# A decode block bound by loading: fewer VectorE instructions, and w_down's row results summed by f32 products

## The chip, the cores and the metric

The kernel runs on one core of a Trainium2 chip. The metric is device time in microseconds (us) of one execution, the median of several runs. A profile comes from one execution. Its span leaves out part of the measured time, so spans and times are never mixed below.

Names used: PE is TensorE's matmul, PEld its weight load (they overlap: 320.5 and 208.1 us busy in a span of 437.8), DVE is VectorE, ACT ScalarE, POOL GpSimd, SP the engine that issues the loads. A "load" is one transfer from HBM; the trace records 16 landings for each of those of weights and cache, and the page counts 16 DMA engines.

## The reference

One decoding step of a transformer block: adaptive layernorm, attention of one query token over a cache of 65,536 positions (4 key/value heads, 32 query heads), then a gated FFN.

```python
def reference(A_x, A_k_cache, A_v_cache, A_wq, A_wo, B_x, B_w_gate, B_w_up, B_w_down, c, w_mod):
    mod = (_silu(c) @ w_mod).reshape(c.shape[0], 6, 1, -1)      # sa, ca, ga, sb, cb, gb
    h = _layernorm(x) * (1 + ca) + sa
    x = x + ga * attention(h)        # k_cache, v_cache: [1, 4, 65536, 128] bf16, 67 MB each
    h = _layernorm(x) * (1 + cb) + sb
    return x + gb * ((_gelu(h @ w_gate) * (h @ w_up)) @ w_down)  # w_down: [3584, 1024]
```

There is one token, so every weight and every cache entry is used once. 185.6 MB must be read.

## The kernel before

The kernel is written engine by engine. Each engine has a program of its own, and semaphores tie the engines together. The parts that the change and the argument touch follow; cuts are marked `# ...` or `...`; in the diffs below, a line in round brackets says what stands there.

The head: GpSimd builds constants and zeroes buffers; VectorE derives selection matrices, gives 40 semaphores their starting value, and zeroes two pads.

```python
pool.memset(p_row[:, :, :], 0.0)
# ...
v_zero = GP.done(pool.memset(kt_sb[:, 1, :, :], 0.0))       # 128 x 8192 bf16
DVE.wait(t1)
dve.memset(selw[:, :], 0.0)
v = DVE.done(dve.memset(q_buf[:, :, :], 0.0))
# ...
dve.tensor_scalar(selt[:, :].rearrange("p (r h) -> p r h", h=REP), identf[0:REP, 0:REP]..., -scale, None, ALU.mult)
# ...
sites = [a for r in ev for a in r] + ex + m1 + m2 + oc + pc + kfill + vfill
for a in sites:
    dve.sem_inc(a.sem, a.unit)
v_pad = DVE.done(dve.memset(s_pad[:, :, :], 0.0))
v_pads = DVE.done(dve.memset(h_pad[:, :, :], 0.0))
```

The loop: 32 steps of 64 x 128 keys. TensorE transposes K, VectorE and ScalarE copy it out, TensorE forms scores, and a running maximum is taken across partitions with two small f32 products (MT, MB) and several small VectorE operations.

```python
v = DVE.done(dve.tensor_reduce(m_new, sc(j), AX.X, ALU.max))
m1[s].done(dve.scalar_tensor_tensor(m_sp[:, j % 2, :], m_new.to_broadcast([P, NR]),
                                    m_run[:, 1 - j % 2:2 - j % 2], rsel[:, :], ALU.max, ALU.mult))
pt["mr"] = DVE.done(dve.tensor_tensor(m_run[...], m_run[...], m_new, ALU.max))
DVE.wait(pt[("MT", j)])
m2[s].done(dve.tensor_reduce(mg[:, j % 2:j % 2 + 1], b6[0:REP, 0:NR], AX.X, ALU.max))
DVE.wait(pt[("MB", j)])
v_mc[j] = DVE.done(dve.tensor_copy(mneg[:, j:j + 1], b6[:, 256:257]))
```

The tail, the w_down product. It has two forms. The "row" form streams 512 columns of w_down past the activations (in the trace a weight load of 128x32 and a product of 128x512), and leaves results in rows that must be turned into columns. The "column" form makes each 128 x 128 block of w_down the stationary operand and streams one column (a weight load of 128x128, a product of 128x1): 8 products for each 128 rows of w_down. The first loads to arrive ("early") use rows, the last four ("late") use columns. Rows are copied out of PSUM, turned by eight f32 transposes, reduced, scaled and added; the column results come on top.

```python
v = row_matvec(place_d, early, o_pad, (v_uc,), ...)
v_rows = both(row_a, 2, P)                              # PSUM -> SBUF, f32, on VectorE and ScalarE
v = turn(tr_ps, P, row_a, plain, P, v_rows)             # 8 f32 transposes of 128 x 128
v = DVE.done(dve.tensor_reduce(t_dn.unsqueeze(2), quads(tr_ps, KD), AX.X, ALU.add))
v = DVE.done(dve.tensor_tensor(t_dn, t_dn, gb_nat[:, :], ALU.mult))
v_base = DVE.done(dve.tensor_tensor(x1_nat[:, :], t_dn, x1_nat[:, :], ALU.add))
v = col_matvec(acc_dn, j_d[len(early):], o_pad[:, :, 0], (), KD)   # 64 products of the late loads
DVE.wait(v, v_base)
```

Of the kernel before, what the change touches and what calls it, by code (L numbers as in the profile page):

```python
# [6 lines left out]
ALU = mybir.AluOpType  # L7
AX = mybir.AxisListType
# [72 lines left out]
def bass_adaLN_cond__gqa_block_cached__geglu_ffn__decode_kernel(  # L81
# [76 lines left out]
    o_acc = sb("o_acc", [P, ROW])  # L158
    o_red = sb("o_red", [P, Hkv, P + 1])
    m_run = sb("m_run", [P, 2])  # L160
    NR = P // REP
    m_sp = sb("m_sp", [P, 2, NR])
    rsel = sb("rsel", [P, NR])
    mg = sb("mg", [REP, 2])
    selt = sb("selt", [REP, P])
    s_fp = s_pad[:, :, :].rearrange("p k c -> p (k c)").bitcast(dt.float32)
# [85 lines left out]
    def emit_all():  # L252
# [64 lines left out]
        while b < NBF:  # L317
# [12 lines left out]
        m1 = [Site(nc, f"m1_{s}") for s in range(SITES)]  # L330
        m2 = [Site(nc, f"m2_{s}") for s in range(SITES)]
        oc = [Site(nc, f"oc{s}") for s in range(SITES)]
# [12 lines left out]
        v_const = GP.done(pool.affine_select(  # L345
            spread[:, :], spread[:, :], [[1, P + QW - 1]], ALU.not_equal, 1.0, base=1 - QW, channel_multiplier=-QW))
        pool.memset(p_row[:, :, :], 0.0)
        pool.memset(p_sb[:, :, :], 0.0)
        pool.memset(m_sp[:, :, :], 0.0)
        pool.memset(mg[:, :], 0.0)  # L350
        pool.memset(slots[SITES + 1][:, 2 * M6 - SLOT:SLOT], 0.0)
        v_zero = GP.done(pool.memset(kt_sb[:, 1, :, :], 0.0))

        DVE.wait(t1)
        dve.memset(selw[:, :], 0.0)
        v = DVE.done(dve.memset(q_buf[:, :, :], 0.0))
        DVE.wait(v)
        dve.tensor_reduce(
            selw[:, HQ - REP:HQ].unsqueeze(2), identf[:, :].rearrange("p (r h) -> p h r", h=REP), AX.X, ALU.add)
        dve.tensor_reduce(  # L360
            rsel[:, :].unsqueeze(2), identf[:, :].rearrange("p (r h) -> p r h", h=REP), AX.X, ALU.add)
        dve.tensor_scalar(  # L362
            selt[:, :].rearrange("p (r h) -> p r h", h=REP),
            identf[0:REP, 0:REP].unsqueeze(1).to_broadcast([REP, NR, REP]), -scale, None, ALU.mult)
        v = DVE.done(dve.tensor_reduce(
            dm4.unsqueeze(3), identf[:, :].rearrange("p (c b h) -> p c b h", c=NQ, h=REP), AX.X, ALU.add))
        DVE.wait(v)
        v_sel = DVE.done(dve.tensor_reduce(
            dmask[:, :].unsqueeze(2), dm4.rearrange("p c b -> p b c"), AX.X, ALU.add))

        sites = [a for r in ev for a in r] + ex + m1 + m2 + oc + pc + kfill + vfill
        for a in sites:
            dve.sem_inc(a.sem, a.unit)

        v_pad = DVE.done(dve.memset(s_pad[:, :, :], 0.0))
        v_pads = DVE.done(dve.memset(h_pad[:, :, :], 0.0))
        PE.wait(t1, (c_sem, 32))
# [12 lines left out]
        v = DVE.done(dve.tensor_scalar(sg_col[:, :], th_col[:, :], 0.5, 0.5, ALU.mult, ALU.add))  # L390
        DVE.wait(v, v_pads)
        v_s = DVE.done(dve.tensor_tensor(s_pad[:, :, 0], c_col[:, :], sg_col[:, :], ALU.mult))

        def col_matvec(bank, jobs, rhs, ready, nblk):

            PE.wait(*ready)
            tok = None
            first = True
            for (jb, view, k0, nk) in jobs:
                PE.wait(jb.tok)  # L400
                ins = None
                for kk in range(nk):
                    for j in range(nblk):
                        ins = pe.matmul(
                            bank[:, j:j + 1], view[:, kk, j * P:(j + 1) * P], rhs[:, k0 + kk:k0 + kk + 1],
                            start=first, stop=True, skip_group_check=True,
                        )
                        first = False
                tok = PE.done(ins)
                release(jb, tok)  # L410
            return tok
# [150 lines left out]

        for s in range(SITES):
            v_q = DVE.done(q_set(s, 0))

# [20 lines left out]
        def pe_step(i, off=0):  # L586
# [48 lines left out]
            def MT():  # L635
                j = i - 1
                if not 0 <= j < NC:
                    return
                pwait(m1[j % SITES], j, it)
                ins = None  # L640
                if emit:
                    ins = pe.matmul(  # L642
                        b6[0:REP, 0:NR], selw[:, HQ - REP:HQ], m_sp[:, j % 2, :], start=True, stop=True)
                pt[("MT", j - off)] = PE.done(ins)

            def MB():
                j = i - 1
                if not 0 <= j < NC:
                    return
                pwait(m2[j % SITES], j, it)  # L650
                ins = None
                if emit:
                    ins = pe.matmul(  # L653
                        b6[:, 256:257], selt[:, :], mg[:, j % 2:j % 2 + 1],
                        start=True, stop=True,
                    )
                pt[("MB", j - off)] = PE.done(ins)

# [51 lines left out]
            MT()  # L710
            MB()

# [3 lines left out]
        def others_step(i):  # L716
# [11 lines left out]
            def OC():  # L728
# [3 lines left out]
                g, first, last = j // NCH, j % NCH == 0, j % NCH == NCH - 1  # L732
                z = o_red[:, g, P:P + 1]
                DVE.wait(pt[("PV", j)], v_x[j], pt.get("z"), pt.get("OC"))
                if first:
                    v = oc[j % SITES].done(dve.tensor_copy(o_acc[:, :], b7[:, :]))
                    pt["z"] = DVE.done(dve.tensor_copy(z, zr[:, j:j + 1]))
                else:
                    v = oc[j % SITES].done(dve.scalar_tensor_tensor(  # L739
                        o_acc[:, :], o_acc[:, :], al[:, j:j + 1], b7[:, :], ALU.mult, ALU.add))  # L740
                    pt["z"] = DVE.done(dve.scalar_tensor_tensor(z, z, al[:, j:j + 1], zr[:, j:j + 1], ALU.mult, ALU.add))
                pt["OC"] = v
                if last:
                    ov = o_acc[:, :].rearrange("p (b d) -> p b d", b=NB)
                    DVE.wait(v)
# [11 lines left out]
            if 0 <= j < NC:  # L757
                s, first = j % SITES, j % NCH == 0
                DVE.wait(pt[("QK", j)])
                if first:  # L760
                    pt["mr"] = v = DVE.done(dve.tensor_reduce(m_run[:, j % 2:j % 2 + 1], sc(j), AX.X, ALU.max))
                    DVE.wait(v)
                    m1[s].done(dve.tensor_scalar(
                        m_sp[:, j % 2, :], rsel[:, :], m_run[:, j % 2:j % 2 + 1], None, ALU.mult))
                else:
                    v = DVE.done(dve.tensor_reduce(m_new, sc(j), AX.X, ALU.max))  # L766
                    DVE.wait(v, pt["mr"])
                    m1[s].done(dve.scalar_tensor_tensor(  # L768
                        m_sp[:, j % 2, :], m_new.to_broadcast([P, NR]), m_run[:, 1 - j % 2:2 - j % 2],
                        rsel[:, :], ALU.max, ALU.mult))  # L770
                    pt["mr"] = DVE.done(dve.tensor_tensor(
                        m_run[:, j % 2:j % 2 + 1], m_run[:, 1 - j % 2:2 - j % 2], m_new, ALU.max))
                if j + SITES < NC and (j + SITES) // NCH != j // NCH:
                    q_set(s, (j + SITES) // NCH)
                DVE.wait(pt[("MT", j)])
                m2[s].done(dve.tensor_reduce(  # L776
                    mg[:, j % 2:j % 2 + 1], b6[0:REP, 0:NR], AX.X, ALU.max))
                DVE.wait(pt[("MB", j)])
                v_mc[j] = DVE.done(dve.tensor_copy(mneg[:, j:j + 1], b6[:, 256:257]))
            jt = i - 2  # L780
# [39 lines left out]
        for g in range(Hkv):  # L820
            ins = pe.matmul(
                b6[0:HQ, 0:P + 1], selw[:, HQ - REP * (g + 1):HQ - REP * (g + 1) + QD], o_red[:, g, :],
                start=g == 0, stop=g == Hkv - 1)
        v = PE.done(ins)
        DVE.wait(v)
        v = DVE.done(dve.reciprocal(rz[:, :], b6[0:HQ, P:P + 1]))
        DVE.wait(v)
# [91 lines left out]
        v_rows = both(row_a, 2, P)  # L919
        v = turn(tr_ps, P, row_a, plain, P, v_rows)  # L920
        DVE.wait(v)
        v = DVE.done(dve.tensor_reduce(t_dn.unsqueeze(2), quads(tr_ps, KD), AX.X, ALU.add))
        DVE.wait(v)
        v = DVE.done(dve.tensor_tensor(t_dn, t_dn, gb_nat[:, :], ALU.mult))
        DVE.wait(v)
        v_base = DVE.done(dve.tensor_tensor(x1_nat[:, :], t_dn, x1_nat[:, :], ALU.add))
        v = col_matvec(acc_dn, j_d[len(early):], o_pad[:, :, 0], (), KD)
        DVE.wait(v, v_base)
        v = DVE.done(dve.tensor_tensor(t_dn, acc_dn, gb_nat[:, :], ALU.mult))
# [42 lines left out]
```

## Time and profile before

439.15 us (439.04 to 439.38, six runs).

| reading | value | view |
|---|---|---|
| span | 437.8 us | page |
| bytes read, mean rate | 185.6 MB, 424 GB/s | page |
| VectorE busy | 50% | page |
| TensorE's waits for K loads in the loop | 28.5 us | waits |

First, lines of the page: DMA busy tenths and GB/s in 40 slices of the span, then three DMA queues (packets, MB, share of 16 engines' span).

```profile
DMA  8999999999999999999999999999999999999994
GB/s 358 433 420 437 436 442 433 430 427 431 434 434 434 432 431 432 431 431 431 431 431 431 431 431 434 432 443 440 440 431 431 431 428 421 439 423 443 414 428 204
q1 hardware_dynamic: 7904, 185.60, 98.6%
q8 instruction: 8, 0.13, 0.1%
q14 instruction: 5, 0.04, 0.0%
```

The rate hardly moves from the second slice to the last but one. The kernel is bound by loading.

The view of waits, TensorE's for K (engine and line, what it waited for, us in all, times, longest):

```profile
PE kt_ps L604 <- DMA slots<-in_A_k_cache_dram: 28.5, 12, 3.7
```

TensorE waits for loads in the loop, not loads for TensorE.

The timeline at the head (start, length, engine, line, operation; in brackets how long the engine had been idle and for whom):

```profile
3.11 12.32 DVE L362 TENSOR_SCALAR selt<-identf 8x128 f32<-8x128 f32 x1
8.44 6.92 POOL L352 MEMSET kt_sb<- 128x8192 bf16 x1
19.27 0.17 DVE L375 MEMSET s_pad<- 128x128 uint32 x1 [3.62 <-issue]
20.97 7.00 PE L427 MATMUL kt_ps<-slots,s_pad 128*32 128x512 bf16 x72
```

VectorE's tiny scaling into `selt` takes 12.32 us and ends at 15.43, when GpSimd's last memset does (15.36). Semaphore increments fill 15.65 to 19.27. The first w_mod products start at 20.97.

The timeline at the tail:

```profile
430.06 1.05 PE L427 MATMUL kt_ps<-slots,p_row 128*32 128x512 bf16 x8 [0.54 <-DMA slots<-in_B_w_down_dram]
431.18 0.69 DVE L845 COPY kt_sb<-kt_ps 128x512 f32<-128x512 f32 x1 [6.76 <-PE kt_ps L427]
431.93 1.97 PE L488 MATMUL sc_ps<-identf,kt_sb 128*128 128x128 f32 x8 [0.82 <-DVE kt_sb L845]
433.69 1.89 PE L404 MATMUL b<-p_row,slots 128*128 128x1 bf16 x64
435.62 0.17 DVE L929 TENSOR_TENSOR kt_sb<-b,gb_nat 128x8 f32<-128x8 f32 x1 [1.09 <-PE b L404]
```

The last early load is used at 430.06, rows are copied by 431.87, the transposes' weight loads run until 433.5, and the late column products end at 435.58.

### The profile page before, as it was taken

The numbers are of one execution on the slowest core, as the hardware profiler recorded it, in microseconds if no ns is written. First come the engines' busy times: TensorE is split into PE (matmuls) and PEld (weight loads), VectorE is DVE, ScalarE is ACT, GpSimd is POOL, SyncE is SP. The second block draws the span as 40 slices with busy tenths as digits, with TensorE's granted clock in tenths as the row PEclk, the third lists the DMA queues.
The fourth block names the chain that finished last, engine by engine and source line by source line (L and its number), as shares of the span: only waits on it lengthen the run. The fifth ranks groups of instructions, "written<-read, shape, count | busy, mean of one in ns | idle before, by whom it ended". The sixth has DMA issues, their size and how long they took to land.

```text
span 437.8 us, 8748 instructions
## 1 busy us (share of the span) xinstructions
PE 320.5 (73%) x3950; PEld 208.1 (48%) x3950; DVE 218.4 (50%) x407; ACT 111.8 (26%) x165; POOL 15.7 (4%) x20
## 2 busy tenths in 40 slices
PE   0156669879896887979697896979888695575466
PEld 0022336656564555655465564655556463232223
DVE  7501024656583746657375674647566475321101
ACT  1000001443332513433333343333235334000000
POOL 9400000000000000000000000000000000000000
PEclk9995558988896968999698898879889999577655
DMA  8999999999999999999999999999999999999994
GB/s 358 433 420 437 436 442 433 430 427 431 434 434 434 432 431 432 431 431 431 431 431 431 431 431 434 432 443 440 440 431 431 431 428 421 439 423 443 414 428 204
DMA packets 7937, 185.78 MB, mean 424 GB/s; under 512 B 882, under 2 KB 882, under 8 KB 1268
## 3 DMA queue, kind: packets, MB, share of 16 engines
q1 hardware_dynamic: 7904, 185.60, 98.6%
q8 instruction: 8, 0.13, 0.1%
q14 instruction: 5, 0.04, 0.0%
q10 hardware_dynamic: 20, 0.01, 0.0%
HBM read 185.60 MB, written 0.00 MB: 424 GB/s over the span
## 4 chain that ended last, share of the span: by engine, by line
DMA 54%; PE 32%; DVE 11%; issue 2%; ACT 1%; POOL 0%; DVEq 0%; POOLq 0%
DMA slots<-in_A_k_cache_dram 43%; PE kt_ps L604 15%; DMA slots<-in_B_w_down_dram 7%; PE b L687 5%; DMA slots<-in_A_v_cache_dram 4%; PE sc_ps L626 4%; PE kt_ps L427 3%; DVE selt L362 3%; DVE kt_sb L726 2%; DVE s_pad L766 1%; DVE o_red L749 1%; PE sc_ps L668 1%; PE sc_ps L488 1%; PE b L653 1%; DVE o_acc L739 1%
## 5 line engine op out<-in xcount | busy, mean ns | idle before, releaser
L604 PE MATMUL kt_ps<-ident,slots 128*128 128x128 bf16 x2048 | 156.6, 237 | 29.2 <-DMA slots<-in_A_k_cache_dram 28.5
L726 DVE COPY kt_sb<-kt_ps 128x2048 bf16<-128x2048 bf16 x96 | 117.5, 1224 | 91.6 <-PE kt_ps L604 87.6
L604 PEld LDWEIGHTS kt_ps<-ident,slots 128*128 128x128 bf16 x2048 | 134.0, 107 | 56.7 <-issue 39.9
L726 ACT ACTIVATE kt_sb<-kt_ps 128x2048 bf16<-128x2048 bf16 x32 | 60.1, 1877 | 28.7 <-PE kt_ps L604 28.7
L784 ACT ACTIVATE p_sb<-sc_ps 128x512 bf16<-128x512 bf16 x32 | 19.1, 597 | 179.8 <-PE sc_ps L668 179.8
L626 PE MATMUL sc_ps<-kt_sb,q_buf 128*32 128x512 bf16 x528 | 51.5, 425 | 0.0
L687 PE MATMUL b<-slots,p_sb 128*32 128x512 bf16 x560 | 43.8, 442 | 4.4 <-DMA slots<-in_A_v_cache_dram 3.7
L427 PE MATMUL kt_ps<-slots,h_pad 128*32 128x512 bf16 x176 | 19.9, 590 | 18.4 <-DMA slots<-in_B_w_up_dram 7.1
L739 DVE SCALAR_TENSOR_TENSOR o_acc<-o_acc,s_pad,b 128x512 f32<-128x512 f32 x28 | 20.9, 748 | 14.9 <-PE b L687 14.8
L687 PEld LDWEIGHTS b<-slots,p_sb 128*32 128x32 bf16 x560 | 16.4, 109 | 20.9 <-issue 8.3
L790 ACT ACTIVATE p_row<-sc_ps,s_pad 128x512 bf16<-128x512 f32 x32 | 21.7, 677 | 0.0
L642 PE MATMUL b<-m_sp,selw 128*8 128x16 f32 x66 | 6.9, 180 | 18.5 <-DVE m_sp L768 16.8
L427 PEld LDWEIGHTS kt_ps<-slots,h_pad 128*32 128x32 bf16 x176 | 6.4, 131 | 29.3 <-issue 11.1
L845 DVE COPY kt_sb<-kt_ps 128x512 f32<-128x512 f32 x4 | 2.8, 692 | 34.4 <-PE kt_ps L427 34.4
L766 DVE TENSOR_REDUCE s_pad<-sc_ps 128x1 f32<-128x512 f32 x28 | 19.0, 680 | 0.0
L653 PE MATMUL b<-mg,selt 8*128 8x1 f32 x66 | 12.5, 256 | 8.2 <-DVE mg L776 8.2
L626 PEld LDWEIGHTS sc_ps<-kt_sb,q_buf 128*32 128x32 bf16 x528 | 11.0, 95 | 12.5 <-issue 4.9
L488 PE MATMUL sc_ps<-identf,kt_sb 128*128 128x128 f32 (+1 forms) x56 | 11.7, 378 | 5.4 <-DVE kt_sb L845 3.2
L653 PEld LDWEIGHTS b<-mg,selt 8*128 8x128 f32 x66 | 9.6, 182 | 11.8 <-DVE mg L776 11.7
L847 ACT ACTIVATE kt_sb<-kt_ps 128x512 f32<-128x512 f32 (+1 forms) x4 | 2.4, 595 | 49.8 <-PE kt_ps L427 49.8
L668 PEld LDWEIGHTS sc_ps<-ident,p_row 128*128 128x128 bf16 x136 | 7.8, 98 | 14.9 <-issue 14.4
L470 POOL TENSOR_TENSOR rs<-va,halfneg 128x1 f32<-128x1 f32 x2 | 1.1, 555 | 378.6 <-DVE va L467 378.6
(114 smaller groups left out, 185.6 us busy)
## 6 DMA issues: line engine op xcount, KB each, us to landing
slots<-in_A_k_cache_dram SPq DMA_DIRECT2D x16, 4096.0 KB, 22.3
slots<-in_A_v_cache_dram SPq DMA_DIRECT2D x16, 4096.0 KB, 23.3
slots<-in_w_mod_dram SPq DMA_DIRECT2D x4, 3072.0 KB, 20.2
slots<-in_A_wq_dram SPq DMA_DIRECT2D x2, 4096.0 KB, 34.0
slots<-in_A_wo_dram SPq DMA_DIRECT2D x4, 2048.0 KB, 26.4
slots<-in_B_w_gate_dram SPq DMA_DIRECT2D x2, 3584.0 KB, 31.0
slots<-in_B_w_up_dram SPq DMA_DIRECT2D x2, 3584.0 KB, 30.4
slots<-in_B_w_down_dram SPq DMA_DIRECT2D x2, 2048.0 KB, 35.0
```

The costliest lines, as they stand in the source:

```text
L362: dve.tensor_scalar(selt[:, :].rearrange("p (r h) -> p r h", h=REP), identf[0:REP, 0:REP].unsqueeze(1).to_broadcast([REP, NR, REP]), -scal ...
L427: ins = pe.matmul(out, pad[:, k, :], view[:, kk, c0:c0 + ROW], start=k <= last_k[0], stop=k >= last_k[1], skip_group_check=True,)
L488: ins = pe.transpose(dst[:, i * w:i * w + n], src[:, a], identf[0:src.shape[0], 0:n])
L604: ins = pe.transpose(kt_ps[:, half * 2048 + t * P:half * 2048 + (t + 1) * P], j_k[i - i % KU].view[:, i % KU * CH + b * TB + t, :], ident[ ...
L626: ins = pe.matmul(sc(j)[QD * g:QD * (g + 1), :], q_buf[:, j % SITES, QD * b:QD * (b + 1)], kt_sb[:, j % 2, n:n + w, :].rearrange("p n d -> ...
L653: ins = pe.matmul(b6[:, 256:257], selt[:, :], mg[:, j % 2:j % 2 + 1], start=True, stop=True,)
L687: ins = pe.matmul(b7[QD * c:QD * (c + 1), :].rearrange("p (b d) -> p b d", b=NB), p_sb[:, s, c * P + QD * g:c * P + QD * (g + 1)], v[:, NQ ...
L726: ev[i % SITES][b].done(act.activation(dst, src, ACT.Copy) if E_ is AC else dve.tensor_copy(dst, src))
L739: v = oc[j % SITES].done(dve.scalar_tensor_tensor(o_acc[:, :], o_acc[:, :], al[:, j:j + 1], b7[:, :], ALU.mult, ALU.add))
L766: v = DVE.done(dve.tensor_reduce(m_new, sc(j), AX.X, ALU.max))
L784: pc[jt % SITES].done(act.activation(p_sb[:, jt % SITES, :], sc_bf[:, o:o + ROW], ACT.Copy))
L790: v_x[j] = ex[s].done(act.activation(p_row[:, j % 2, :], sc(j), ACT.Exp, bias=mneg[:, j:j + 1], scale=scale, accum_out=zr[:, j:j + 1],))
```

## The change

Its intent: VectorE should run fewer instructions (485 before by the traces, those on semaphores counted too). The running maximum becomes one operation that works on all 16 spread columns, and one f32 product with a 128 x 128 operand replaces MT and MB. The sums of the softmax are taken by one scan per head instead of one operation per step. Memsets and semaphore increments move to GpSimd. In the tail, the rows are no longer turned: eight f32 products of the rows with a column of ones add them straight into the column sums, with the first late load's products ahead of them.

```diff
-        dve.memset(selw[:, :], 0.0)
-        v = DVE.done(dve.memset(q_buf[:, :, :], 0.0))
+        pool.memset(s_pad[:, :, :], 0.0)
+        pool.memset(h_pad[:, :, :], 0.0)
+        pool.memset(q_buf[:, :, :], 0.0)
+        v_pads = GP.done(pool.memset(selw[:, :], 0.0))
...
-        for a in sites:
-            dve.sem_inc(a.sem, a.unit)
+        for a in [a for r in ev for a in r] + ex + m1 + oc + pc + kfill + vfill:
+            pool.sem_inc(a.sem, a.unit)
...
-                        b6[0:REP, 0:NR], selw[:, HQ - REP:HQ], m_sp[:, j % 2, :], start=True, stop=True)
+                        b6[:, 0:NR], selt[:, :], m_sp[:, j % 2, :], start=True, stop=True)
-            def MB(): ...
...
-                    pt["z"] = DVE.done(dve.scalar_tensor_tensor(z, z, al[:, j:j + 1], zr[:, j:j + 1], ALU.mult, ALU.add))
                 if last:
+                    dve.tensor_tensor_scan(
+                        o_red[:, g, P:P + ZW], al[:, j - ZW + 1:j + 1], zr[:, j - ZW + 1:j + 1],
+                        zr[:, j - ZW:j - ZW + 1], ALU.mult, ALU.add)
...
-                    m1[s].done(dve.scalar_tensor_tensor(
-                        m_sp[:, j % 2, :], m_new.to_broadcast([P, NR]), m_run[:, 1 - j % 2:2 - j % 2],
-                        rsel[:, :], ALU.max, ALU.mult))
-                    pt["mr"] = DVE.done(dve.tensor_tensor(...))
+                    v = m1[s].done(dve.scalar_tensor_tensor(
+                        m_sp[:, j % 2, :], rsel[:, :], m_new, m_sp[:, 1 - j % 2, :], ALU.mult, ALU.max))
...
-                m2[s].done(dve.tensor_reduce(mg[:, j % 2:j % 2 + 1], b6[0:REP, 0:NR], AX.X, ALU.max))
-                DVE.wait(pt[("MB", j)])
-                v_mc[j] = DVE.done(dve.tensor_copy(mneg[:, j:j + 1], b6[:, 256:257]))
+                v_mc[j] = DVE.done(dve.tensor_reduce(mneg[:, j:j + 1], b6[:, 0:NR], AX.X, ALU.min))
...
-        v = turn(tr_ps, P, row_a, plain, P, v_rows)
-        (reduction, product with gb, sum with x1)
-        v = col_matvec(acc_dn, j_d[len(early):], o_pad[:, :, 0], (), KD)
+        late = j_d[len(early):]
+        col_matvec(acc_dn, late[:1], o_pad[:, :, 0], KD, True)
+        PE.wait(*v_rows)
+        for j, a in enumerate(plain):
+            pe.matmul(
+                acc_dn[:, j:j + 1], row_a[:, a], ones1[:, :], start=False, stop=True, skip_group_check=True)
+        v = col_matvec(acc_dn, late[1:], o_pad[:, :, 0], KD, False)
```

More of the change, by code (lines that the diff above doesn't have):

```diff
@@ L158, in bass_adaLN_cond__gqa_block_cached__geglu_ffn__decode_kernel @@
     o_acc = sb("o_acc", [P, ROW])
-    o_red = sb("o_red", [P, Hkv, P + 1])
-    m_run = sb("m_run", [P, 2])
+    ZW = NCH - 1
+    o_red = sb("o_red", [P, Hkv, P + ZW])
     NR = P // REP
@@ L163, in bass_adaLN_cond__gqa_block_cached__geglu_ffn__decode_kernel @@
     rsel = sb("rsel", [P, NR])
-    mg = sb("mg", [REP, 2])
-    selt = sb("selt", [REP, P])
+    selt = sb("selt", [P, P])
     s_fp = s_pad[:, :, :].rearrange("p k c -> p (k c)").bitcast(dt.float32)
@@ L330, in emit_all @@
         m1 = [Site(nc, f"m1_{s}") for s in range(SITES)]
-        m2 = [Site(nc, f"m2_{s}") for s in range(SITES)]
         oc = [Site(nc, f"oc{s}") for s in range(SITES)]
@@ L349, in emit_all @@
         pool.memset(m_sp[:, :, :], 0.0)
-        pool.memset(mg[:, :], 0.0)
         pool.memset(slots[SITES + 1][:, 2 * M6 - SLOT:SLOT], 0.0)
+        for a in [a for r in ev for a in r] + ex + m1 + oc + pc + kfill + vfill:
+            pool.sem_inc(a.sem, a.unit)
         v_zero = GP.done(pool.memset(kt_sb[:, 1, :, :], 0.0))
-        DVE.wait(t1)
-        dve.memset(selw[:, :], 0.0)
-        v = DVE.done(dve.memset(q_buf[:, :, :], 0.0))
-        DVE.wait(v)
+        DVE.wait(v_pads)
         dve.tensor_reduce(
@@ L361, in emit_all @@
             rsel[:, :].unsqueeze(2), identf[:, :].rearrange("p (r h) -> p r h", h=REP), AX.X, ALU.add)
-        dve.tensor_scalar(
-            selt[:, :].rearrange("p (r h) -> p r h", h=REP),
-            identf[0:REP, 0:REP].unsqueeze(1).to_broadcast([REP, NR, REP]), -scale, None, ALU.mult)
         v = DVE.done(dve.tensor_reduce(
@@ L367, in emit_all @@
         DVE.wait(v)
+        dve.tensor_scalar(
+            selt[:, :].rearrange("p (r h) -> p r h", h=REP),
+            selw[:, HQ - REP:HQ].unsqueeze(1).to_broadcast([P, NR, REP]), -scale, None, ALU.mult)
         v_sel = DVE.done(dve.tensor_reduce(
             dmask[:, :].unsqueeze(2), dm4.rearrange("p c b -> p b c"), AX.X, ALU.add))
-        sites = [a for r in ev for a in r] + ex + m1 + m2 + oc + pc + kfill + vfill
-        for a in sites:
-            dve.sem_inc(a.sem, a.unit)
-        v_pad = DVE.done(dve.memset(s_pad[:, :, :], 0.0))
-        v_pads = DVE.done(dve.memset(h_pad[:, :, :], 0.0))
         PE.wait(t1, (c_sem, 32))
@@ L390, in emit_all, with col_matvec @@
         v = DVE.done(dve.tensor_scalar(sg_col[:, :], th_col[:, :], 0.5, 0.5, ALU.mult, ALU.add))
-        DVE.wait(v, v_pads)
+        DVE.wait(v)
         v_s = DVE.done(dve.tensor_tensor(s_pad[:, :, 0], c_col[:, :], sg_col[:, :], ALU.mult))
-        def col_matvec(bank, jobs, rhs, ready, nblk):
-            PE.wait(*ready)
+        def col_matvec(bank, jobs, rhs, nblk, first):
             tok = None
-            first = True
             for (jb, view, k0, nk) in jobs:
@@ L561, in q_set @@
             return dve.tensor_copy(q_diag(s), q_col[:, g * REP:(g + 1) * REP].unsqueeze(1).to_broadcast([P, NB, REP]))
-        for s in range(SITES):
-            v_q = DVE.done(q_set(s, 0))
+        v_q = DVE.done(dve.tensor_copy(
+            q_buf[:, :, :].rearrange("p s (m c) -> p s m c", c=QS)[:, :, :, 0:REP],
+            q_col[:, 0:REP].unsqueeze(1).unsqueeze(1).to_broadcast([P, SITES, NB, REP])))
         sc_bf = sc_ps[:, :].bitcast(dt.bfloat16)
@@ L642, in MT @@
                     ins = pe.matmul(
-                        b6[0:REP, 0:NR], selw[:, HQ - REP:HQ], m_sp[:, j % 2, :], start=True, stop=True)
+                        b6[:, 0:NR], selt[:, :], m_sp[:, j % 2, :], start=True, stop=True)
                 pt[("MT", j - off)] = PE.done(ins)
-            def MB():
-                j = i - 1
-                if not 0 <= j < NC:
-                    return
-                pwait(m2[j % SITES], j, it)
-                ins = None
-                if emit:
-                    ins = pe.matmul(
-                        b6[:, 256:257], selt[:, :], mg[:, j % 2:j % 2 + 1],
-                        start=True, stop=True,
-                    )
-                pt[("MB", j - off)] = PE.done(ins)
             def PT():
@@ L710, in pe_step @@
             MT()
-            MB()
         v_mc = {}
@@ L732, in OC @@
                 g, first, last = j // NCH, j % NCH == 0, j % NCH == NCH - 1
-                z = o_red[:, g, P:P + 1]
-                DVE.wait(pt[("PV", j)], v_x[j], pt.get("z"), pt.get("OC"))
+                DVE.wait(pt[("PV", j)])
                 if first:
                     v = oc[j % SITES].done(dve.tensor_copy(o_acc[:, :], b7[:, :]))
-                    pt["z"] = DVE.done(dve.tensor_copy(z, zr[:, j:j + 1]))
                 else:
@@ L759, in others_step @@
                 DVE.wait(pt[("QK", j)])
+                v = DVE.done(dve.tensor_reduce(m_new, sc(j), AX.X, ALU.max))
+                DVE.wait(v)
                 if first:
-                    pt["mr"] = v = DVE.done(dve.tensor_reduce(m_run[:, j % 2:j % 2 + 1], sc(j), AX.X, ALU.max))
-                    DVE.wait(v)
-                    m1[s].done(dve.tensor_scalar(
-                        m_sp[:, j % 2, :], rsel[:, :], m_run[:, j % 2:j % 2 + 1], None, ALU.mult))
-                else:
-                    v = DVE.done(dve.tensor_reduce(m_new, sc(j), AX.X, ALU.max))
-                    DVE.wait(v, pt["mr"])
-                    m1[s].done(dve.scalar_tensor_tensor(
-                        m_sp[:, j % 2, :], m_new.to_broadcast([P, NR]), m_run[:, 1 - j % 2:2 - j % 2],
-                        rsel[:, :], ALU.max, ALU.mult))
-                    pt["mr"] = DVE.done(dve.tensor_tensor(
-                        m_run[:, j % 2:j % 2 + 1], m_run[:, 1 - j % 2:2 - j % 2], m_new, ALU.max))
+                    v = m1[s].done(dve.tensor_scalar(m_sp[:, j % 2, :], rsel[:, :], m_new, None, ALU.mult))
+                else:
+                    v = m1[s].done(dve.scalar_tensor_tensor(
+                        m_sp[:, j % 2, :], rsel[:, :], m_new, m_sp[:, 1 - j % 2, :], ALU.mult, ALU.max))
                 if j + SITES < NC and (j + SITES) // NCH != j // NCH:
@@ L775, in others_step @@
                 DVE.wait(pt[("MT", j)])
-                m2[s].done(dve.tensor_reduce(
-                    mg[:, j % 2:j % 2 + 1], b6[0:REP, 0:NR], AX.X, ALU.max))
-                DVE.wait(pt[("MB", j)])
-                v_mc[j] = DVE.done(dve.tensor_copy(mneg[:, j:j + 1], b6[:, 256:257]))
+                v_mc[j] = DVE.done(dve.tensor_reduce(mneg[:, j:j + 1], b6[:, 0:NR], AX.X, ALU.min))
             jt = i - 2
@@ L821, in emit_all @@
             ins = pe.matmul(
-                b6[0:HQ, 0:P + 1], selw[:, HQ - REP * (g + 1):HQ - REP * (g + 1) + QD], o_red[:, g, :],
+                b6[0:HQ, 0:P + ZW], selw[:, HQ - REP * (g + 1):HQ - REP * (g + 1) + QD], o_red[:, g, :],
                 start=g == 0, stop=g == Hkv - 1)
@@ L825, in emit_all @@
         DVE.wait(v)
-        v = DVE.done(dve.reciprocal(rz[:, :], b6[0:HQ, P:P + 1]))
+        v = DVE.done(dve.reciprocal(rz[:, :], b6[0:HQ, P + ZW - 1:P + ZW]))
         DVE.wait(v)
@@ L919, in emit_all @@
         v_rows = both(row_a, 2, P)
-        v = turn(tr_ps, P, row_a, plain, P, v_rows)
-        DVE.wait(v)
-        v = DVE.done(dve.tensor_reduce(t_dn.unsqueeze(2), quads(tr_ps, KD), AX.X, ALU.add))
-        DVE.wait(v)
-        v = DVE.done(dve.tensor_tensor(t_dn, t_dn, gb_nat[:, :], ALU.mult))
-        DVE.wait(v)
-        v_base = DVE.done(dve.tensor_tensor(x1_nat[:, :], t_dn, x1_nat[:, :], ALU.add))
-        v = col_matvec(acc_dn, j_d[len(early):], o_pad[:, :, 0], (), KD)
-        DVE.wait(v, v_base)
+        late = j_d[len(early):]
[5 more added lines that the diff above has]
+        v = col_matvec(acc_dn, late[1:], o_pad[:, :, 0], KD, False)
+        DVE.wait(v, v_xn)
         v = DVE.done(dve.tensor_tensor(t_dn, acc_dn, gb_nat[:, :], ALU.mult))
```

## The prediction

> **What bounds the kernel.** Loading. The page's DMA rows give 185.6 MB read; from the second of the forty slices to the last but one every slice moves 414 to 443 GB/s with the DMA engines 90% busy or more. 185.6 MB at about 431 GB/s is 430.6 us (my estimate), of a span of 437.8. The DMA issuer waits for TensorE to free slots (157 us and 152 us in the view of waits), but the rate never sinks, so enough transfers are queued. VectorE is busy only 50%. Only about 2 us before the stream and the stretch after it are open to change. In stretches of a quarter microsecond the rate falls at 431.5 us and is near nothing after 433.0: the last 4.8 us are the tail.
>
> **The loop (maxima, sums, one small matmul and one VectorE hop fewer).** The timeline shows an 8x128 f32 product of 0.38 us and VectorE operations of about 0.15 us saved per step. Many sit in the chain of waits, but that chain goes back each time to a K load 19 to 23 us long. The saving becomes a longer wait for that load. Worth 0.
>
> **The head.** The scaling that makes selt took 12.3 us on VectorE (3.11 to 15.43), ending as GpSimd's last memset ended (15.36). [...] Then 3.6 us are semaphore increments. Moving these to GpSimd opens a gap between its memsets, and the s_pad product may come 5 to 10 us earlier. But the second wq load issued at about 24.9 and K at 26.3 were queued behind transfers running until about 33 and later, so no load starts earlier. Worth 0.
>
> **The tail.** Before: early w_down products end 431.15, rows are copied by 431.88, eight f32 transposes run 431.93 to 433.48 (pitch 0.22 us, clock 0.50), then 64 bf16 column products at 0.03 us end 435.6. After: 32 column products fill the copy's gap (about 1.0 us, to 432.15). Then eight f32 products with a 128x128 stationary operand replace the transposes, but the trace shows every true f32 product as two instructions (66 for 33 calls, 8 for 4), each with its own weight load. The layernorm's, with the same 128x128 operand and two columns, took 0.50 us for two loads early (0.25 each) and 0.30 us at 393.4 (full clock). So 16 passes at 0.20 to 0.25 us: about 3.5 us, to 435.7; then the other 32 column products, 0.95 us, to 436.6. That is 1.0 us later than before. [...] here the granted clock went 0.50 to 1.00 about 5 us into the run from 384.2; TensorE now works without a gap from 430.06, so the last passes may be faster. I take off a little: +0.8 us.
>
> **Prediction: 440.0 us, range 438.7 to 441.3.** Faster by over 2%: 0.01; within 2%: 0.98; slower: 0.01.
>
> **What would show it.** DMA rate near 431 GB/s and its end near 433 us, unchanged; first w_mod product earlier with no earlier end of loading; 16 f32 instructions of about 0.2 us in the tail; final column products ending near 436.4.
>
> **What would make it wrong.** f32 passes at 0.12 us or less (then 1 us faster than before, about 438.3); some stretch where the queue really ran dry and a quicker loop fills it (then faster).

Its sum: 0 for the loop, 0 for the head, and for the tail 1.0 less 0.2, taken off for the clock step from 0.50 to 1.00 that its own trace shows at about 389.5: +0.8 us, from 439.15 to 440.0.

## The result and the profile after

439.81 us (439.72 to 440.00, six runs) against 439.15. Ratio 1.0015, 95% interval 1.0002 to 1.0028. A ratio here is the mean time of one kernel's runs over that of the other's of the same rounds, so it is not quite the ratio of the quoted medians. The time is inside the predicted range and 0.2 us from its centre. The profile shows that two of the steps that led there were wrong, in opposite directions.

Lines of the page after, as before:

```profile
GB/s 355 430 435 439 435 432 429 429 424 433 433 430 433 431 433 430 433 436 430 436 439 433 436 428 430 430 439 430 436 430 430 430 426 429 444 428 434 415 430 173
q8 instruction: 8, 0.13, 0.1%
q14 instruction: 4, 0.03, 0.0%
```

The rate is the same. The waits for K, TensorE:

```profile
PE kt_ps L597 <- DMA slots<-in_A_k_cache_dram: 47.9, 14, 5.1
```

They grew from 28.5 to 47.9 us: the loop's shorter chain has become waiting, as predicted. The head:

```profile
4.30 12.26 DVE L365 TENSOR_SCALAR selt<-selw 128x128 f32<-128x128 f32 x1
6.11 3.50 POOL L352 MEMSET slots<- 128x4096 bf16 x1
9.57 6.91 POOL L355 MEMSET kt_sb<- 128x8192 bf16 x1
9.64 6.92 DVE L378 COPY c_col<-b 128x8 f32<-128x8 f32 x1
17.96 5.43 PE L419 MATMUL kt_ps<-slots,s_pad 128*32 128x512 bf16 x48
```

The gap between GpSimd's memsets, which the prediction expected from the semaphore increments, is not there: one memset ends at 9.61 and the next starts at 9.57. `selt` still takes 12.26 us, and three copies of 128 x 8 out of PSUM last 6.8 to 6.9 us: they come after `selt` in VectorE's program and end when it does, at 16.56. The first w_mod products start at 17.96, 3.0 us earlier, which is about what the increments had cost VectorE (3.6 us). The tail:

```profile
428.56 1.05 PE L419 MATMUL kt_ps<-slots,p_row 128*32 128x512 bf16 x8 [1.41 <-DMA slots<-in_B_w_down_dram]
429.68 0.69 DVE L815 COPY kt_sb<-kt_ps 128x512 f32<-128x512 f32 x1 [6.82 <-PE kt_ps L419]
431.01 1.01 PE L396 MATMUL b<-p_row,slots 128*128 128x1 bf16 x32 [1.40 <-DMA slots<-in_B_w_down_dram]
431.89 3.55 PE L894 MATMUL b<-ones,kt_sb 128*128 128x1 f32 x16
435.30 0.99 PE L396 MATMUL b<-p_row,slots 128*128 128x1 bf16 x32
436.33 0.17 DVE L898 TENSOR_TENSOR kt_sb<-b,gb_nat 128x8 f32<-128x8 f32 x1 [5.96 <-PE b L396]
```

Two things stand out. The f32 sums take 3.55 us, 16 instructions at about 0.22. That was predicted. But the last early load is used at 428.56, which is 1.50 us sooner than before. All later loads are sooner too. The next two fences give TensorE's first use of some loads, before and after (in brackets the wait for the load).

```profile
270.87 1.89 PE L604 MATMUL kt_ps<-ident,slots 128*128 128x128 bf16 x16 [3.68 <-DMA slots<-in_A_k_cache_dram]
291.22 1.89 PE L604 MATMUL kt_ps<-ident,slots 128*128 128x128 bf16 x16 [2.43 <-DMA slots<-in_A_k_cache_dram]
400.94 3.60 PE L427 MATMUL kt_ps<-slots,h_pad 128*32 128x512 bf16 x28 [3.19 <-DMA slots<-in_B_w_gate_dram]
```

```profile
271.02 1.89 PE L597 MATMUL kt_ps<-ident,slots 128*128 128x128 bf16 x16 [5.04 <-DMA slots<-in_A_k_cache_dram]
290.44 1.89 PE L597 MATMUL kt_ps<-ident,slots 128*128 128x128 bf16 x16 [3.82 <-DMA slots<-in_A_k_cache_dram]
399.35 2.49 PE L419 MATMUL kt_ps<-slots,h_pad 128*32 128x512 bf16 x28 [3.22 <-DMA slots<-in_B_w_gate_dram]
```

Until 271 us the kernels are level. Between 271 and 291 the changed one gains 0.9 us, and between 291 and 400 another 0.8. Yet the rate of loading was the same. What differs is not how much arrives but when a load is complete.

The trace has 16 landings for each of the 53 loads of weights and cache, and it has each packet of the DMA queues. The page counts 16 DMA engines, and I read each landing as that of one of them, though the trace does not name the engine. On that reading the distance from the first landing to the last is how far the slowest DMA engine has fallen behind the fastest. Worked out from the trace's records of landings, for some loads (us):

```
          before                             after
first     lag of the 14th, 15th, last       first     lag of the 14th, 15th, last
269.1     1.66  1.68  1.69                  269.0     1.91  1.99  2.01
278.8     1.70  1.71  2.63                  278.6     1.95  2.01  2.02
375.7     1.68  1.69  2.48                  375.5     1.91  1.92  1.98
380.5     1.71  1.72  3.47                  380.3     1.93  1.94  2.00
431.7     1.68  1.69  3.32 (lands 434.99)   431.5     1.88  1.90  1.97 (lands 433.49)
```

Of the 1.50 us between the last landings, 1.34 are this lag; most of the rest is there from the first load on. Before, one DMA engine drops back by 0.9 us at 279 and by 1.0 us at 380, and makes up less than 0.2 us of either by the end. Why it does not catch up was not shown. At these times, 278.9 and 380.3, the trace has an 8 KB packet in q14, the second of the instruction queues. When the packets of q14 began, with the number of VectorE instructions that had begun by then:

```
before  q14 at  23.4 (63)  150.2 (171)  174.0 (195)  278.9 (321)  380.3 (446)
after   q14 at   9.1 (7)    92.2 (51)   149.2 (94)   252.8 (178)
```

The fetches at 23.4, 174.0, 278.9 and 380.3 before, and at 92.2 and 252.8 after, are 125 to 132 VectorE instructions apart: VectorE fetched four times before, and twice after. The one at 150 (149) occurs in both and goes by ScalarE's count (48 begun in both); the one at 9.1 came after GpSimd had been given 39 more instructions. Whose fetch is whose is inferred from these counts; in the padded kernels below VectorE's come at similar counts: 64 to 76, 188 to 198, 315 to 325, 449 and 574.

### The profile page after: what moved, and what is told of

Same layout as the page of the kernel before. It is cut to its first block, busy times and chain, and to the rows that moved or that the text cites. A ratio compares the mean times of both kernels' runs of the same rounds, so it can differ in the third digit from the quotient of the medians. Undisturbed runs are those within 1.5% of the kernel's fastest.

```text
span 438.6 us, 8499 instructions
## 1 busy us (share of the span) xinstructions
PE 305.5 (70%) x3892; PEld 203.4 (46%) x3892; DVE 206.9 (47%) x309; ACT 111.8 (25%) x165; POOL 16.8 (4%) x23
## 4 chain that ended last, share of the span: by engine, by line
DMA 56%; PE 31%; DVE 10%; issue 1%; ACT 1%; POOL 0%; POOLq 0%; SPq 0%
DMA slots<-in_A_k_cache_dram 44%; PE kt_ps L597 16%; DMA slots<-in_B_w_down_dram 8%; PE b L667 4%; DMA slots<-in_A_v_cache_dram 4%; PE sc_ps L619 4%; PE kt_ps L419 3%; DVE selt L365 3%; DVE kt_sb L705 2%; DVE s_pad L739 1%; DVE o_red L728 1%; PE b L894 1%; PE sc_ps L648 1%; PE b L635 1%; DVE o_acc L716 1%
## 5 line engine op out<-in xcount | busy, mean ns | idle before, releaser
L597 PE MATMUL kt_ps<-ident,slots 128*128 128x128 bf16 x2048 | 156.8, 238 | 48.6 <-DMA slots<-in_A_k_cache_dram 47.9
L597 PEld LDWEIGHTS kt_ps<-ident,slots 128*128 128x128 bf16 x2048 | 136.1, 108 | 74.2 <-issue 41.8
L667 PE MATMUL b<-slots,p_sb 128*32 128x512 bf16 x560 | 40.1, 411 | 5.3 <-DMA slots<-in_A_v_cache_dram 4.6
L419 PE MATMUL kt_ps<-slots,h_pad 128*32 128x512 bf16 x176 | 18.0, 544 | 20.9 <-DMA slots<-in_B_w_up_dram 8.6
L635 PE MATMUL b<-m_sp,selt 128*128 128x16 f32 x66 | 13.0, 272 | 18.2 <-DVE m_sp L744 16.5
L667 PEld LDWEIGHTS b<-slots,p_sb 128*32 128x32 bf16 x560 | 15.5, 104 | 20.2 <-issue 5.2
L739 DVE TENSOR_REDUCE s_pad<-sc_ps 128x1 f32<-128x512 f32 x32 | 21.8, 680 | 0.0
L635 PEld LDWEIGHTS b<-m_sp,selt 128*128 128x128 f32 x66 | 9.8, 188 | 23.7 <-DVE m_sp L744 21.4
L419 PE MATMUL kt_ps<-slots,s_pad 128*32 128x512 bf16 x96 | 10.9, 517 | 7.4 <-DMA slots<-in_w_mod_dram 7.4
L648 PE MATMUL sc_ps<-ident,p_row 128*128 128x128 bf16 x136 | 13.7, 224 | 0.2 <-ACT p_row L760 0.2
```

Source lines behind the costliest of these rows:

```text
L419: ins = pe.matmul(out, pad[:, k, :], view[:, kk, c0:c0 + ROW], start=k <= last_k[0], stop=k >= last_k[1], skip_group_check=True,)
L597: ins = pe.transpose(kt_ps[:, half * 2048 + t * P:half * 2048 + (t + 1) * P], j_k[i - i % KU].view[:, i % KU * CH + b * TB + t, :], ident[ ...
L635: ins = pe.matmul(b6[:, 0:NR], selt[:, :], m_sp[:, j % 2, :], start=True, stop=True)
L648: ins = pe.transpose(sc_bf[:, o:o + P], p_row[:, j % 2, c * P:(c + 1) * P], ident[:, :])
L667: ins = pe.matmul(b7[QD * c:QD * (c + 1), :].rearrange("p (b d) -> p b d", b=NB), p_sb[:, s, c * P + QD * g:c * P + QD * (g + 1)], v[:, NQ ...
```

## The experiments

Theory F (formed after the first four runs): the end of loading moved because VectorE fetches its instructions twice less often, and each fetch sets one DMA engine back for good. Rival L: the loop's shorter chain brought the gain. Rival H: the head's earlier start brought it. At first I still held that the tail was the whole difference; the first four runs were made for that. The runs were made on three chips; the kernel before took 439.12 to 439.17 us on each.

### The tail of before in the changed kernel (tail_old)

```diff
-        late = j_d[len(early):]
-        (first late load, f32 sums, other late loads)
+        v = turn(tr_ps, P, row_a, plain, P, v_rows)
+        (reduction, product, sum; then all late loads)
```

> The changed kernel with the tail of before (eight f32 transposes, reduction, product, sum), so only the head and the loop are changed. Theory 1 (the whole difference is the f32 sums of the tail; head and loop are worth 0 because loading bounds them): ratio to before 1.000, between 0.9992 and 1.0008, final column products end about 435.6 us. Rival (the head or the loop costs or gives something, and the tail covers it): ratio off by 0.001 or more, for example 1.0015 if the tail is innocent.

Measured: 437.58 us, ratio 0.9965 (0.9951 to 0.9978). The timeline of its tail:

```profile
428.59 1.05 PE L419 MATMUL kt_ps<-slots,p_row 128*32 128x512 bf16 x8 [1.35 <-DMA slots<-in_B_w_down_dram]
430.46 1.97 PE L480 MATMUL sc_ps<-identf,kt_sb 128*128 128x128 f32 x8 [0.81 <-DVE kt_sb L815]
432.22 1.89 PE L396 MATMUL b<-p_row,slots 128*128 128x1 bf16 x64
```

Theory 1 (the tail is the whole difference) fell: head and loop are worth 1.5 us, not 0. The tail of before starts here at 428.59 instead of 430.06 and runs as it ran then. This is also the fastest kernel together with sums_bf16, 0.35% faster than before.

### The new tail in the kernel before (tail_new_only)

The reverse: only the tail's part of the diff.

> The kernel before with the new tail alone. Theory 1: about 439.8 us, ratio 1.0015 (1.001 to 1.0025), 16 f32 passes of about 0.22 us in the tail. Rival (tail innocent): ratio 1.000.

Measured: 441.37 us, ratio 1.0052 (1.0039 to 1.0066), above what both theories expected. The timeline:

```profile
429.94 1.06 PE L425 MATMUL kt_ps<-slots,p_row 128*32 128x512 bf16 x8 [1.39 <-DMA slots<-in_B_w_down_dram]
431.06 0.69 DVE L843 COPY kt_sb<-kt_ps 128x512 f32<-128x512 f32 x1 [6.75 <-PE kt_ps L425]
432.39 1.01 PE L402 MATMUL b<-p_row,slots 128*128 128x1 bf16 x32 [1.40 <-DMA slots<-in_B_w_down_dram]
433.27 3.55 PE L922 MATMUL b<-ones,kt_sb 128*128 128x1 f32 x16
436.68 0.99 PE L402 MATMUL b<-p_row,slots 128*128 128x1 bf16 x32
```

The tail alone costs 2.2 us, from both sides: 441.37 - 439.13 here, and 439.81 - 437.58 between the changed kernel and tail_old. The change is the sum of -1.5 and +2.2. The first late load was taken at 432.39, after a wait of 1.40 us, though the rows had been ready since 431.75.

### The f32 sums twice (sums_twice)

```diff
+        for j, a in enumerate(plain):
+            pe.matmul(tr_ps[:, j:j + 1], row_a[:, a], ones1[:, :], start=True, stop=True, skip_group_check=True)
```

> The changed kernel with the eight f32 sums done twice (the second time into a bank that nobody reads). Theory 1, all of the sums lie on the last chain at 0.22 us a pass: 3.5 us more than the changed kernel, so about 443.3 us, ratio 1.0095. If half of them hide behind the last load: about 441.5 us. If TensorE's clock doubles in between: about 441.8 us.

Measured: 443.20 us, ratio 1.0093 (1.0078 to 1.0108), 3.4 us over the changed kernel.

```profile
431.81 3.55 PE L894 MATMUL b<-ones,kt_sb 128*128 128x1 f32 x16
435.22 3.55 PE L897 MATMUL sc_ps<-ones,kt_sb 128*128 128x1 f32 x16
```

The second set costs what the first costs, so all of it is on the last chain. TensorE was busy without a gap from 430.94 to 439.63, 8.7 us, and its granted clock stayed at half, 0.50 in every stretch of 2 us from 430 to 440. In the changed kernel it was 0.50 too, from 431.01 to 436.29. So the third case of the expectation, a clock that doubles as it did in the kernel before at about 389.5 (0.50 to 1.00), did not occur.

### The sums in bf16 (sums_bf16)

```diff
-        v_rows = both(row_a, 2, P)
+        row_b = kt_sb[:, 1, 0:KD, :].rearrange("p a b -> p (a b)")
+        v_rows = both(row_b, 2, P)
-                acc_dn[:, j:j + 1], row_a[:, a], ones1[:, :], ...
+                acc_dn[:, j:j + 1], row_b[:, a], ones_b[:, :], ...
```

> The changed kernel with the rows copied to bf16 and summed against bf16 ones (a rounding more; may still pass the comparison). Theory 1 (the time is the price of two f32 passes with their weight loads): eight instructions of about 0.03 us in place of sixteen of 0.22, after which the last load (about 433.2 us) bounds: 437.0 us, ratio 0.995. Rival (the price is the order, TensorE waiting for the late jobs): no more than 0.5 us faster than the changed kernel.

Measured: 437.53 us, ratio 0.9963 (0.9949 to 0.9976), results still within the comparison's tolerance. That is 2.3 us faster than the changed kernel, so the rival (no more than 0.5) falls. The weight loads of the sums in the changed kernel and here:

```profile
431.86 3.49 PEld L894 LDWEIGHTS b<-ones,kt_sb 128*128 128x128 f32 x16
```

```profile
432.00 0.29 PEld L897 LDWEIGHTS b<-ones_b,kt_sb 128*128 128x128 bf16 x8
433.67 0.38 PE L398 MATMUL b<-p_row,slots 128*128 128x1 bf16 x8 [0.23 <-DMA slots<-in_B_w_down_dram]
```

16 f32 weight loads take 3.49 us, eight bf16 ones 0.29: 0.22 against 0.036 each, and half as many. With the sums gone TensorE waits for the last load, used at 433.67. The expected 437.0 was 0.5 us too low.

### The head alone (head_only)

The kernel before with the diff's lines on memsets and semaphore increments, loop and tail untouched.

> The kernel before with the head of the change alone: memsets and the 40 semaphore increments on GpSimd, loop and tail untouched, some 45 VectorE instructions fewer. Theory F (instruction fetches): the trace of before has VectorE fetching 8 KB of instructions at 23.4, 174.0, 278.9 and 380.3 us, about 128 instructions apart, and at each one DMA engine falls back by some 0.9 us for the rest of the run; 45 fewer drop the fetch at 380.3, so the lag of the last DMA engine ends at 2.6 instead of 3.4 us: 438.3 us, ratio 0.998. Rival L (the gain of 1.5 us comes from the shorter chain in the loop): 439.1 us, ratio 1.000. Rival H (the earlier start of the head brings the whole gain): 437.6 us.

Measured: 438.30 us, ratio 0.9982 (0.9969 to 0.9996), as theory F expected. Its "at each one" goes beyond the trace of before: the last engine's lag grows by 0.9 us at 278.9 and by 1.0 at 380.3, by 0.7 at 23.4 (loads of 17.3 and 24.5), and does not grow at 174.0 (1.77 us at the load of 172.3, 1.75 at that of 182.0). The trace has VectorE at 441 instructions and three fetches that fit its count (93.2, 203.0, 306.7); the lag of the last DMA engine ends at 2.47 us. Rivals L and H, as put, expected 439.1 and 437.6.

### VectorE padded with idle instructions (pad_96, pad_192, pad_320)

In tail_old, semaphore increments that nobody waits for are spread over the loop, 3, 6 or 10 a step:

```diff
             OC()
             E(2)
+            if i < NC:
+                for _ in range(6):
+                    dve.sem_inc(idle_sem, 1)
```

> tail_old (437.6 us) with 96 semaphore increments on VectorE that nobody waits for, three in each step of the loop. Theory F: three fetches of VectorE instead of two, lag of the last DMA engine about 2.6 us in place of 2.0, so 438.1 to 438.3 us. Rival L or H: nothing depends on their number, 437.6 us.

> tail_old with 192 such increments, six in each step, about as many VectorE instructions as before the change. Theory F: four fetches, lag about 3.4 us as before, 439.0 us, ratio to before 1.000. Rival L or H: 437.6 us, ratio 0.9965.

> tail_old with 320 such increments, ten in each step. Theory F: five fetches, lag about 4.3 us, 439.8 us. Rival L or H: 437.6 us; if VectorE's extra 0.9 us a step were felt in the loop, the waits for K would be gone from the trace.

Measured: 438.43, 439.19 and 439.95 us, each 0.1 to 0.2 us over what theory F expected; ratios 0.9985 (0.9971 to 0.9999), 1.0002 (0.9988 to 1.0016) and 1.0018 (1.0005 to 1.0032). The page's line of the fetching queue, first pad_192, then pad_320 (the last two of VectorE's fetches of pad_320 are at 290.8 and 362.5):

```profile
q14 instruction: 6, 0.05, 0.0%
```

```profile
q14 instruction: 7, 0.06, 0.0%
```

All kernels that share the tail of before, from the traces (the last two columns: lag of the slowest DMA engine at the last load, and its landing; a packet of q14 at 436.3 us in tail_old, after loading had ended, is not counted):

```
kernel       VectorE        its fetches          time     lag    last
             instructions                        us       us     landing us
tail_old     317            2                    437.58   2.01   433.54
pad_96       413            3                    438.43   2.67   434.29
head_only    441            3                    438.30   2.47   434.10
before       485            4                    439.15   3.32   434.99
pad_192      509            4                    439.19   3.44   435.00
pad_320      637            5                    439.95   4.39   436.00
```

From the third on, time goes by the number of fetches, 0.7 to 0.9 us for each, and not by the kind of loop: "before" with the long chain and pad_192 with the short one take the same time. Nor did the increments use up the loop's slack: TensorE's waits for K are 48.7 and 45.7 us in all in pad_192 and pad_320, beside 46.3 in tail_old. Rivals L and H fall as explanations of the gain. The tail of before hangs on the last early load, which carries the same lag: its last share lands at 430.01 before and at 428.55 in tail_old.

The first two fetches should cost nothing, though no kernel with fewer was run: in pad_320 the slowest engine lagged 1.86 us after VectorE's second fetch (load of 220.7), and the next one 1.78. The others' lag grew mostly between 47 and 97 us (before, the 14th landing's from 0.31 us at the load of 41.6 to 1.71 at that of 94.8), while q8 had five 16 KB packets; whether these caused it was not tested.

### The same 192 increments on GpSimd (pad_pool_192)

> tail_old with the 192 increments on GpSimd instead of VectorE. GpSimd then fetches once or twice more (it has 69 instructions in tail_old). If its fetches fall on the DMA engine that serves VectorE's too: like pad_192, 438.4 to 439.2 us. If on another one that has room below the lag of 2.0 us: 437.6 us for one fetch, at most 438.2 for two. If it is the increments themselves, whoever does them, that cost time in pad_192: 439.2 us.

Measured: 437.64 us, ratio 0.9964 (0.9951 to 0.9978). GpSimd has 261 instructions, and one more packet of q14, at 32.2 us. The lag there rises to 1.7 us, but by the end it is 2.03, as in tail_old. So 192 increments as such cost nothing; GpSimd ran them all by 34.0 us, though, and not over the loop as VectorE did, so for their place only the waits for K above speak. If that packet is GpSimd's, one more fetch of another instruction stream stayed below the lag of 2.01 us that tail_old has without it.

### The loop slowed (loop_slow)

```diff
-                    ins = pe.matmul(b6[:, 0:NR], selt[:, :], m_sp[:, j % 2, :], start=True, stop=True)
+                    for _ in range(4):
+                        ins = pe.matmul(b6[:, 0:NR], selt[:, :], m_sp[:, j % 2, :], start=True, stop=True)
```

> The changed kernel with the f32 product that spreads the maximum done four times in each step, 0.25 us each on the chain of the step, some 24 us in all 32 steps. Theory F and the prediction's own step (the loop waits for K, its chain is worth 0): 439.8 us, the waits for K about 20 us shorter in sum than the 48 us of the changed kernel. Rival L: later by a microsecond and more.

Measured: 439.92 us, ratio 1.0017 (1.0003 to 1.0031), beside 439.81 and 1.0015 for the changed kernel. The waits for K:

```profile
PE kt_ps L597 <- DMA slots<-in_A_k_cache_dram: 27.5, 12, 3.4
```

The repeated product kept TensorE busy for 35.6 us in place of 13.0. This came out of the waits, 47.9 to 27.5 us, and the time did not move. The prediction's reading of the loop's chain was right.

### The sums ahead of the late loads (sums_first)

```diff
-        col_matvec(acc_dn, late[:1], o_pad[:, :, 0], KD, True)
         PE.wait(*v_rows)
         (the f32 sums, the first now with start=True)
-        v = col_matvec(acc_dn, late[1:], o_pad[:, :, 0], KD, False)
+        v = col_matvec(acc_dn, late, o_pad[:, :, 0], KD, False)
```

> The changed kernel with the f32 sums ahead of the late column products. In its trace the rows are ready at 430.4 and TensorE waits until 431.0 for the first late job, which it takes first. If that order is part of the tail's cost: sums 430.4 to 433.9, then 64 column products to 435.8, so about 0.6 us less than the changed kernel, 439.2 us. If the sums alone are the cost: 439.8 us.

Measured: 439.26 us, ratio 1.0002 (0.9989 to 1.0016), 0.55 less than the changed kernel.

```profile
430.41 3.57 PE L893 MATMUL b<-ones,kt_sb 128*128 128x1 f32 x16 [0.81 <-DVE kt_sb L815]
433.84 1.84 PE L396 MATMUL b<-p_row,slots 128*128 128x1 bf16 x64
```

This splits the tail's 2.2 us. Beside tail_old, whose transposes start within 0.05 us of these sums, the column products start at 433.84 instead of 432.22: 1.6 us is the price of 16 f32 passes over 8 transposes. The other 0.6 is the order: in the changed kernel TensorE waited for the first late load until 431.01, while the sums, ready since 430.4, stood behind it in its program.

### All of w_down in column form (all_columns)

```diff
-        early = [a for a in j_d if a[2] < NROW * UE]
-        (row products, copies, sums)
+        PE.wait(v_uc)
+        v = col_matvec(acc_dn, j_d, o_pad[:, :, 0], KD, True)
```

> The changed kernel with all of w_down done as column products (224 of 0.03 us), so that there are no rows to copy, to turn or to sum. What is loaded first is done while the rest is loading; after the last landing (about 433.5 us) one job of 8 products is left. If the tail is then bound by the last landing: 437.3 us, ratio 0.9958. If TensorE falls behind the loads (28 times 0.24 us is 6.7 us of work in the last 11 us): not under 438 us.

Measured: 437.89 us, ratio 0.9970 (0.9956 to 0.9983). TensorE keeps up and the last job waits for the last landing:

```profile
433.54 0.38 PE L396 MATMUL b<-p_row,slots 128*128 128x1 bf16 x8 [0.23 <-DMA slots<-in_B_w_down_dram]
```

Expected were 437.3 us; it is no better than tail_old, whose interval overlaps. What is left at the end is the last landing, at 433.49, and the steps that follow one another from 433.54 to the span's end at 436.2.

## Why the prediction was right, and where it was wrong

- **"What bounds the kernel. Loading."** Right: 430 GB/s before and after, and loop_slow's 20 us vanished in waits.
- **"Its end near 433 us, unchanged."** Wrong. The last landing was at 434.99 before and 433.49 after. I had read the end of loading from the mean rate, which was near nothing after 433.0 (25 GB/s up to 433.5); but the last of 16 landings came 1.6 us after the 15th (434.99 and 433.37), and TensorE used a load only after the last: the last early one at 430.06 after 430.01 before, at 428.56 after 428.51 in the changed kernel. A mean over engines hides that.
- **"The loop ... Worth 0" and "The head ... Worth 0."** Wrong in sum by 1.5 us (tail_old), though right about the chains. The head's removed VectorE instructions are worth 0.8 us (head_only), and the loop's the rest, 0.7 by subtraction. The step that failed is "the saving becomes a longer wait for that load": true for time on the engine (the waits for K grew from 28.5 to 47.9 us), but with fewer VectorE instructions q14 also had four packets instead of five, and the lag at the last load was 1.97 us instead of 3.32. The prediction looked at no fetch queue.
- **"Moving these to GpSimd opens a gap between its memsets."** Wrong: no gap; w_mod's products started 3.0 us earlier, less than the 5 to 10 that it allowed. Again `selt` ended at 16.56, as GpSimd's last memset did (16.48); what ties the two was not tested.
- **"16 passes at 0.20 to 0.25 us."** Right: 0.22.
- **The tail, "+0.8 us".** Mis-sized: 2.2 us. The failed term is "32 column products fill the copy's gap (about 1.0 us, to 432.15)". It took for granted that the first late load was there at 431.15. With the loop of before it was taken at 432.39 (tail_new_only). And the 0.2 us taken off for a rising clock was not to be had. In the kernel before, the run from 384.2 had the granted clock at 1.00 from about 389.5; here it stayed at 0.50 through 5.3 us of gapless work (431.01 to 436.29), and through 8.7 in sums_twice (430.94 to 439.63). Why it rose there and not here was not shown.
- **The sum.** +0.8 predicted, +0.7 measured: -1.5 that was not foreseen and 1.4 too little for the tail cancel. The number was right by luck.

What stays open: why an 8 KB fetch, 0.31 us as a packet, sets its DMA engine back by 0.9 to 1.0 us; and which DMA engine it is, since the trace does not name them. That VectorE's fetches all fall on one is inferred from the lag of the last engine, which in pad_320 rises by 1.0 us at each of the last three fetches, 0.8 to 0.9 net of what it makes up until the next.

## What to carry to other kernels

Where loading is the bound and never pauses, look at when the slowest DMA engine lands (434.99 us in the kernel before), not at the mean rate (near nothing there from 433.0), and count the instructions of each engine's program: about 128 fewer on VectorE spared one fetch and 0.7 to 0.9 us here, as long as more than two were left, and smaller steps nothing that showed (413 and 441 instructions, or 485 and 509, took the same time within 0.15 us). Before replacing transposes by f32 products, count the instructions and weight loads that an f32 product becomes (two of each here, 0.22 us a pass, beside one of each for a transpose), and put work that is ready ahead of work that waits for a load (0.6 us here). Test the parts of a change apart even if the total comes out as predicted: here dropping the change's tail gave 437.58 us, better than both kernels.
